# Five weight steps in six slots instead of seven, two a slot in the first sixteen, and one empty step behind each weight load

## The chip, the core and the metric

The kernel runs on one core of a Trainium2 chip. The metric is the device time of one execution in microseconds (us). The kernel before was run three times: 621.59, 623.79 and 624.48 us, median 623.79 us.

## What is computed

The reference is an attention with a hash mask, followed by a gated convolutional feed-forward layer:

```
q_bucket, k_bucket = sign bits of q @ proj and k @ proj, as numbers
scores = where(q_bucket == k_bucket, scale * q @ k.T, -1e9)
attn   = softmax(scores);  x = attn @ v          # B 4, H 8, S 768, D 64
gate   = sigmoid(causal conv of x, 5 taps, conv_w)
out    = (gate * (x @ w_val)) @ w_out            # 512 x 512 weights
```

`w_val`, `w_out` and `conv_w` come as 64-bit floats, which the chip's engines don't compute with. The kernel reads them as pairs of 32-bit integers and converts each weight into a high part and a low part of single precision (`wv[0]`, `wv[1]`, `wo[0]`, `wo[1]`), since the products are made of three partial products (high by high, high by low, low by high).

## The kernel before

**Units and slots.** There are 32 units (4 batches by 8 heads), and each has six tiles of 128 queries, 192 tiles in all. The main loop (L490) takes one pass per tile; a pass is called a slot here, and slot k is the pass that computes the exponentials of tile k (L290). In the slot, in this order: ScalarE (ACT) copies the transposed probabilities of tile k-4 out of PSUM (L323); VectorE (DVE) takes the row maxima of tile k (L272) and two small factors (L278, L282); GpSimd (POOL) normalises tile k-2 (L305); TensorE (PE) computes the scores of tile k+1 (L266); ACT computes the exponentials; then come the steps of the side work, and at the end PE transposes tile k-3 (L314). In odd slots PE also multiplies by the values (L337).

**Order.** The order on PE, ACT, DVE and POOL is the order in which the program is written (`manual_schedule`); each engine runs its list strictly in that order, and an instruction that waits holds all behind it. The score tiles have two PSUM buffers, so the scores of tile k+2 wait for the exponentials of tile k. The transposed tiles have two buffers (`tp`), and one tile uses both, so the transposes of a slot wait for ACT's copies of the tile before. SyncE (SP) issues the transfers in a list of its own, also in order.

**Side work.** Generators stand beside the loop, and each `yield` ends a step: `prep` builds the operands of the next unit (POOL L170 and L173, then transfers between partitions, L174 to L182), `early_bits` computes hash bits of later units (L221 loads, L226, L229), `pair_x` does the convolution on DVE (L368), and `load_weights` (L131) converts the weights. There are two `load_weights` generators, which take turns: `weights[0]` first converts `conv_w` and then the parts 0, 2, 4, 6; `weights[1]` converts the parts 1, 3, 5, 7. Parts 0 to 3 are the quarters of `w_val`, parts 4 to 7 those of `w_out`. The first step of each generator runs ahead of the loop.

**The steps of a part.** One part is 128 x 512 values. Its steps are: the load (L137, 512 KB); ACT's absolute value, which is the transfer's first reader (L91); two DVE operations (L93, L94); one DVE operation (L97); two DVE operations (L100, L101); a DVE cast (L109); a POOL subtraction (L111); a POOL addition (L113) and, in the same step, the load of this generator's next part. That is seven steps a part. The loads have two buffers in turn: part 0 takes the second one fresh, and part 3 takes the buffer of part 1 when L113 of part 1 is done. The slots take 1, 0, 2, 0, 2, 2 steps in turn (L515), seven in six slots, and the last step of a part falls in slot 56.

Of the kernel before, what the change touches and what calls it, by code (L numbers as in the profile page):

```python
# [26 lines left out]
def kernel(  # L27
# [11 lines left out]
    B, H, _, S = qk.shape  # L39
# [65 lines left out]
    def split_weight(w, hi, lo):  # L105
        if w.dtype == I32:
            a, d = yield from from_float64(w, op.tile([P, 512], FP32, name="o"))
            yield
            nc.vector.tensor_copy(out=hi, in_=a)  # L109
            yield  # L110
            nc.gpsimd.tensor_tensor(out=a, in0=a, in1=hi.bitcast(FP32), op=ALU.subtract)  # L111
            yield
            nc.gpsimd.tensor_tensor(out=lo, in0=a, in1=d, op=ALU.add)  # L113
        else:
            nc.scalar.copy(out=hi, in_=w)
            yield
            nc.gpsimd.tensor_tensor(out=lo, in0=w, in1=hi.bitcast(FP32), op=ALU.subtract)

    def load_conv():
        if conv_w.dtype == mybir.dt.int64:  # L120
            w = const.tile([P, NP * KW, 2], I32, name="cw64")
            nc.sync.dma_start(out=w, in_=conv_w.bitcast(I32).rearrange("p (n t) -> p n t", t=2))
            t = const.tile([P, NP * KW], FP32, name="cwt")
            yield
            a, d = yield from from_float64(w, t)
            yield
            nc.vector.tensor_tensor(out=cw_sb, in0=d, in1=a, op=ALU.add)
        else:
            nc.sync.dma_start(out=cw_sb, in_=conv_w)

    def load_weights(which):  # L131
        parts = [(src[:, c, :], hl[0][:, c, :], hl[1][:, c, :])
                 for src, hl in ((w_val, wv), (w_out, wo)) for c in range(NP)]
        for src, hi, lo in parts[which::2]:
            if src.dtype == mybir.dt.int64:
                w = wst.tile([P, 512, 2], I32, name="w64")
                nc.sync.dma_start(out=w, in_=src.bitcast(I32).rearrange("p (n t) -> p n t", t=2))  # L137
            else:
                w = wst.tile([P, 512], FP32, name="w32")
                nc.sync.dma_start(out=w, in_=src)  # L140
            yield
            yield from split_weight(w, hi, lo)

    def load_raw(i):
        if i < len(units):
            b, h = units[i]
            raws[i] = raw.tile([P, S], FP32, name="r")
            nc.sync.dma_start(out=raws[i], in_=qk[b, h])

    def load_values(i):  # L150
        b, h = units[i]
        if h % 2 == 0:
            vts[i] = vp.tile([P, KB, P], FP32, name="vt")
            nc.sync.dma_start(out=vts[i], in_=v[b, h // 2])
        else:
            vts[i] = vts[i - 1]
# [81 lines left out]
    def first_prep():  # L238

        r = raws[0]  # L240
        aq, ak, bq, bk = stacks[0] = [stk.tile([P, S], FP32R, name=nm) for nm in ("aq", "ak", "bq", "bk")]
        z = ps_t.tile([P, 512], FP32, name="tp")
        for g in range(4):
            nc.tensor.matmul(out=z[32 * g:32 * g + 2 * NB, 0:HS], lhsT=proj_sb[:, 2 * NB * (g // 2):2 * NB * (g // 2 + 1)],
                             rhs=r[:, HS * (g % 2):HS * (g % 2 + 1)], start=True, stop=True, tile_position=(0, 32 * g))
        nc.scalar.copy(out=aq[0:D], in_=r[0:D])
        nc.vector.tensor_copy(out=bk[D:P], in_=r[D:P])
        nc.vector.tensor_copy(out=ak[0:D], in_=r[D:P])
        nc.gpsimd.tensor_tensor(out=bk[0:D], in0=r[D:P], in1=bk[D:P].bitcast(FP32), op=ALU.subtract)
        for g in (0, 2, 3, 1):  # L250
            if g == 1:
                nc.vector.tensor_tensor(out=bq[D:P], in0=r[0:D], in1=aq[0:D].bitcast(FP32), op=ALU.subtract)  # L252
            nc.vector.tensor_scalar(out=(aq, ak)[g // 2][D:M, HS * (g % 2):HS * (g % 2 + 1)],
                                    in0=z[32 * g:32 * g + 2 * NB, 0:HS],
                                    scalar1=rows_sb[32 * g:32 * g + 2 * NB, 2:3],
                                    scalar2=rows_sb[32 * g:32 * g + 2 * NB, 3:4], op0=ALU.is_ge, op1=ALU.mult)
        nc.scalar.copy(out=bq[0:D], in_=r[0:D])
# [218 lines left out]
    with tc.manual_schedule(engines=ENGINES):  # L476
        for i in range(5):
            load_raw(i)
        load_values(0)
        first_prep()  # L480
        weights = [[load_conv(), load_weights(0)], [load_weights(1)]]
        preps = [first_bits(), prep(1)]
        scores(0)
        next(preps[1])
        step(preps)
        step(weights[0])
        step(weights[1])
        ahead = [early_bits()]
        turn = 0
        for k in range(N + LAG + 1):  # L490
            if 0 <= k - LAG - 1:
                keep_transposed(k - LAG - 1)
            pair = k % 2 == 0 and 0 <= k - 2 < N
            if k < N:
                maxima(k)
            if pair:
                row_sums(k - 2)
            if k < N:
                factors(k)
            if pair:  # L500
                recip(k - 2)
            if 0 <= k - 2 < N:
                normalise(k - 2)
            if k < N:
                shifts(k)
            if k + 1 < N:
                if tiles[k + 1][0] != tiles[k][0]:
                    finish(preps)
                    preps = [prep(tiles[k + 1][0] + 1)]
                scores(k + 1)  # L510
            if k < N:
                exponentials(k)
            if k >= 60 or k % 2:
                step(convs)
            for _ in range((1, 0, 2, 0, 2, 2)[k % 6]):  # L515
                step(weights[turn])
                turn = 1 - turn

            thin = k // 6 % 8 in (7, 0) and k < 186
            for _ in range(3 if cur["gates"] else (1, 0)[k % 2] if thin else 1):  # L520
                step(moes)
            cur["gates"] = max(0, cur["gates"] - 1)
            step(preps)
            if 6 <= k < 60 and k % 6 in (2, 4):
                step(ahead)
            if k % 2:
                step(avs)
                step(avs)
            if 0 <= k - LAG < N:
                transposes(k - LAG)  # L530
        accs[:] = [(ps_m, "m"), (ps_t, "tp"), (ps_s, "s"), (ps_t, "tp"), (ps_s, "s")]
        finish(avs)
        cur["gates"] = 0
        cur["end"] = True
        while convs:
            step(convs)
            step(moes)
        finish(moes)
# [59 lines left out]
```

## Time and profile before

| | |
|---|---|
| median of three runs | 623.79 us |
| span of the profiled execution, first to last instruction | 620.8 us |
| that is below the three runs by | 0.8 to 3.7 us, 3.0 us below the median |
| busy: PE, DVE, ACT, POOL | 94%, 70%, 68%, 64% of the span |

The page gives no time of its own for the profiled execution beside the span; what lies around the span is taken as the 3.0 us to the median. Slot 0 begins at 12.05 us, slot 16 at 53.80, slot 53 at 157.30, slot 65 at 188.48 (the start of L290 in each). The first use of the weights on PE is at 188.1 us (L399), of the output weights at 224.9 us (L424).

### The profile page before, as it was taken

The page shows a single profiled execution, that of the slowest core. Times are in us where ns is not written, and L with a number is a line of the kernel's source. Part 1 is how long each engine was busy: PE and PEld are TensorE (multiplying, and loading weights), DVE is VectorE, ACT ScalarE, POOL GpSimd, SP SyncE. Part 2 cuts the span into 40 slices and gives each one's busy share as a digit, 9 for nine tenths or more (in the row PEclk, how much of TensorE's full clock was granted, in tenths as well). Part 3 has the DMA queues.
Part 4 walks back from the last instruction along what each step waited for, and adds up shares of the span by engine and source line. Part 5 has one row for each costly group of instructions (what it writes and reads, how often), then busy time and mean ns, then how long its engine had stood idle before and what let it go on. Part 6 is the DMA issues. An engine that isn't in the chain of part 4 may idle for free.

```text
span 620.8 us, 10648 instructions
## 1 busy us (share of the span) xinstructions
PE 585.5 (94%) x3496; PEld 423.4 (68%) x3496; DVE 437.6 (70%) x1017; ACT 421.4 (68%) x881; POOL 395.6 (64%) x373
## 2 busy tenths in 40 slices
PE   5789898989999999999999999999999999999997
PEld 2655565555657777776767777777667877775895
DVE  5869798998975866668575867569665877665532
ACT  2777777778778666777787676777787766765400
POOL 3576868778766765578564777568764777544321
PEclk9799999999999999999999999999999999999999
DMA  6467666564532235243433234333422213200111
GB/s 227 123 197 199 200 167 208 157 175 118 133 83 68 70 79 142 72 108 82 122 82 107 61 80 126 84 115 82 108 70 78 67 42 91 69 18 1 51 52 51
DMA packets 29031, 64.64 MB, mean 104 GB/s; under 512 B 4937, under 2 KB 10057, under 8 KB 28977
## 3 DMA queue, kind: packets, MB, share of 16 engines
q1 hardware_dynamic: 28832, 63.93, 37.8%
q8 instruction: 28, 0.46, 0.3%
q14 instruction: 27, 0.21, 0.1%
q10 hardware_dynamic: 144, 0.03, 0.0%
HBM read 30.60 MB, written 7.86 MB: 62 GB/s over the span
## 4 chain that ended last, share of the span: by engine, by line
PE 66%; DVE 12%; ACT 12%; DMA 5%; issue 3%; POOL 2%; SPq 1%; ACTq 0%; POOLq 0%; DVEq 0%
PE av L337 17%; PE s L266 16%; PE tp L314 12%; PE m L424 8%; PE m L399 7%; ACT p L290 5%; DVE nm L272 4%; ACT pt L323 3%; ACT x L345 2%; DMA w<-in_w_val_dram 2%; DVE g L368 2%; PE tp L399 1%; PE tp L424 1%; PE s L424 1%; DMA bk<-bq 1%
## 5 line engine op out<-in xcount | busy, mean ns | idle before, releaser
L305 POOL TENSOR_SCALAR p<-p,ri 128x768 f32<-128x768 f32 x192 | 210.5, 1100 | 156.0 <-DVE nb L282 130.8
L272 DVE TENSOR_REDUCE nm<-s 128x1 f32<-128x768 f32 x192 | 182.5, 950 | 61.2 <-PE s L266 61.0
L290 ACT ACTIVATE p<-s,nb,gs 128x768 f32<-128x768 f32 x192 | 192.6, 1003 | 46.2 <-DVE nb L282 41.9
L323 ACT COPY pt<-tp 128x384 f32<-128x384 f32 x384 | 165.7, 485 | 75.3 <-PE tp L314 74.4
L314 PEld LDWEIGHTS tp<-ident,p 128*128 128x128 f32 x1152 | 130.3, 142 | 72.2 <-issue 43.6
L314 PE MATMUL tp<-ident,p 128*128 128x128 f32 x1152 | 164.4, 279 | 2.6 <-ACT pt L323 2.1
L337 PE MATMUL av<-pt,vt 128*64 128x384 f32 x768 | 144.9, 498 | 0.0
L266 PE MATMUL s<-ak,aq 76*128 76x384 f32 x384 | 118.1, 389 | 23.2 <-ACT p L290 19.7
L266 PE MATMUL s<-bk,bq 128*128 128x384 f32 x384 | 101.3, 345 | 0.4 <-DVE bq L252 0.4
L337 PEld LDWEIGHTS av<-pt,vt 128*64 128x64 f32 x768 | 47.0, 136 | 61.5 <-issue 61.4
L266 PEld LDWEIGHTS s<-ak,aq 76*128 76x128 f32 x384 | 59.2, 194 | 38.7 <-ACT p L290 34.6
L368 DVE SCALAR_TENSOR_TENSOR g<-x,cw_sb,g 128x768 f32<-128x768 f32 x64 | 79.4, 1241 | 2.2 <-POOL g L366 2.1
L266 PEld LDWEIGHTS s<-bk,bq 128*128 128x128 f32 x384 | 71.7, 194 | 0.8 <-issue 0.8
L173 POOL TENSOR_TENSOR bq<-r,aq 128x768 fp32r<-128x768 f32 x31 | 59.2, 1909 | 0.1
L410 POOL TENSOR_TENSOR hl<-ht,hh 128x384 fp32r<-128x384 f32 x32 | 32.3, 1009 | 39.5 <-DVE hh L408 39.5
L345 ACT COPY x<-av 64x384 f32<-64x384 f32 x64 | 30.4, 475 | 29.7 <-PE av L337 29.0
L282 DVE TENSOR_SCALAR nb<-nm,gs 128x1 f32<-128x1 f32 x192 | 40.4, 211 | 3.5
L399 PE MATMUL m<-xh,wv 128*128 128x384 f32 x200 | 42.7, 337 | 0.0
L358 POOL TENSOR_TENSOR xl<-x,xh 128x384 fp32r<-128x384 f32 x32 | 33.4, 1059 | 13.8 <-DVE xh L357 13.8
L290 ACT ACTIVATION_READ_ACCUMULATOR p<-s,nb,gs 128x1 f32 x192 | 39.0, 203 | 0.0
L404 DVE TENSOR_TENSOR ht<-m,g 128x384 f32<-128x384 f32 x25 | 13.9, 556 | 35.6 <-PE m L399 29.2
L424 PE MATMUL m<-wo,hh 128*128 128x512 f32 x144 | 38.1, 394 | 0.0
(86 smaller groups left out, 486.9 us busy)
## 6 DMA issues: line engine op xcount, KB each, us to landing
r<-in_qk_dram SPq DMA_DIRECT2D x32, 384.0 KB
vt<-in_v_dram SPq DMA_DIRECT2D x16, 384.0 KB
out_dram<-o SPq DMA_DIRECT2D x24, 256.0 KB
ak<-aq SPq DMA_DIRECT2D x31, 192.0 KB
bk<-aq SPq DMA_DIRECT2D x31, 192.0 KB
bk<-bq SPq DMA_DIRECT2D x31, 192.0 KB
bq<-aq SPq DMA_DIRECT2D x31, 192.0 KB
hh<-in_qk_dram SPq DMA_DIRECT2D x16, 192.0 KB
```

Source lines behind the costliest of these rows:

```text
L173: nc.gpsimd.tensor_tensor(out=bq, in0=r, in1=aq.bitcast(FP32), op=ALU.subtract)
L266: nc.tensor.matmul(out=s[:, hf, 0:HS], lhsT=lq[0:n, qs], rhs=rk[0:n, hf * HS:(hf + 1) * HS], start=n == M, stop=n == P)
L272: nc.vector.tensor_reduce(out=nm, in_=s[:, :, 0:HS], axis=AX.XY, op=ALU.max, negate=True)
L290: nc.scalar.activation(out=p, in_=s[:, :, 0:HS], func=AF.Exp, bias=nb, scale=gs.pop(k), accum_out=sm[:, k % 2, 0:1])
L305: nc.gpsimd.tensor_scalar(out=p, in0=p, scalar1=rcs.pop(k), scalar2=1.0, op0=ALU.mult, op1=ALU.mult)
L314: nc.tensor.transpose(out=tp[:, n * P:(n + 1) * P], in_=p[:, kb * P:(kb + 1) * P], identity=ident)
L323: nc.scalar.copy(out=pt[:, :, qo:qo + P], in_=tp[:, 0:HS].rearrange("p (a b) -> p a b", b=P))
L337: nc.tensor.matmul(out=av[s * D:(s + 1) * D, 0:HS], lhsT=vt[:, kb, hh * D:(hh + 1) * D], rhs=pt[kb // 3][:, kb % 3, :], start=(kb == 0), s ...
L345: nc.scalar.copy(out=x[hh * D:(hh + 1) * D, o:o + HS], in_=av[s * D:(s + 1) * D, 0:HS])
L368: nc.vector.scalar_tensor_tensor(out=g, in0=x[:, k:k + S], scalar=w, in1=g, op0=ALU.mult, op1=ALU.add)
L399: nc.tensor.matmul(out=acc[:, 0:HS], lhsT=wv[wi][:, c, j * P:(j + 1) * P], rhs=xs_[(c, o)][xi], start=(m == 0), stop=(m == 11))
L424: nc.tensor.matmul(out=acc, lhsT=hs[(o, j)][hi][:, tb * P:(tb + 1) * P], rhs=wo[wi][:, j, :], start=(m == 0), stop=(m == 11))
```

## The change

The conversion takes two steps a slot in slots 0 to 15, and from slot 16 on 1, 0, 1, 1, 1, 1 in turn, five in six slots. Behind the load of a part stands a second `yield`, an empty step, so that a part has eight steps and the reader L91 comes one step of its generator later after the load. All lines behind L141 move down by one.

```
@@ -138,6 +138,7 @@
                 w = wst.tile([P, 512], FP32, name="w32")
                 nc.sync.dma_start(out=w, in_=src)
             yield
+            yield
             yield from split_weight(w, hi, lo)
@@ -512,7 +513,7 @@
             if k >= 60 or k % 2:
                 step(convs)
-            for _ in range((1, 0, 2, 0, 2, 2)[k % 6]):
+            for _ in range(2 if k < 16 else (1, 0, 1, 1, 1, 1)[k % 6]):
                 step(weights[turn])
                 turn = 1 - turn
```

Counted out slot by slot, the steps fall like this (only DVE's operations, ACT's L91 and the loads are listed; the number is the part):

```
slot   before                        after
 4     L93/94 of 1                   load 0; L100/101 of 1
 6     L100/101 of 1                 L91 of 0; L111 of 1
 7     -                             L93/94 of 0; L113 of 1; load 3
 8     load 0; L109 of 1             L97 of 0
 9     -                             L100/101 of 0; L91 of 3
10     L91 of 0; L111 of 1           L109 of 0; L93/94 of 3
11     L93/94 of 0; L113, load 3     L111 of 0; L97 of 3
12     L97 of 0                      L113 of 0; load 2; L100/101 of 3
14     L91 of 3; L100/101 of 0       L91 of 2; L111 of 3
15     -                             L93/94 of 2; L113 of 3; load 5
...
20     load 2; L109 of 3             L91 of 5
22     L91 of 2; L111 of 3           L93/94 of 5
26     L91 of 5; L100/101 of 2       L113 of 2; load 4
53     L111 of 6                     L113 of 7
59     -                             L109 of 6
64     -                             L113 of 6, the last step
```

Nothing is added or removed on an engine; PE's list is the same.

ACT in slots 8 to 10, before: L91 here reads `w_425`, part 0.

```order
L290 ACTIVATE p,sm<-s,nb,gs 128x768
L323 COPY pt<-tp 128x3x128 x2
L290 ACTIVATE p,sm<-s,nb,gs 128x768
L323 COPY pt<-tp 128x3x128 x2
L290 ACTIVATE p,sm<-s,nb,gs 128x768
L91 ACTIVATE o<-w_425 128x512
L323 COPY pt<-tp 128x3x128 x2
```

And after, slots 8 to 10, where L91 reads `w_405`, part 3:

```order
L291 ACTIVATE p,sm<-s,nb,gs 128x768
L324 COPY pt<-tp 128x3x128 x2
L291 ACTIVATE p,sm<-s,nb,gs 128x768
L91 ACTIVATE o<-w_405 128x512
L324 COPY pt<-tp 128x3x128 x2
L291 ACTIVATE p,sm<-s,nb,gs 128x768
L324 COPY pt<-tp 128x3x128 x2
```

The L91 whose load stands in this place of SP's list (between `bq<-aq` of unit 2 and the four loads `hh`) comes behind the exponentials of slot 10 before, and behind those of slot 9 after.

POOL from slot 5 on, before: L173 builds `bq` of unit 2, `p` is the normalisation, `w_176` is part 1.

```order
L170 CAST aq<-r 128x768
L305 TENSOR_SCALAR p<-p,ri 128x768
L173 TENSOR_TENSOR bq<-r,aq 128x768
L305 TENSOR_SCALAR p<-p,ri 128x768 x4
L111 TENSOR_TENSOR w_176<-w_176,wv_120 128x512
L305 TENSOR_SCALAR p<-p,ri 128x768
L113 TENSOR_TENSOR wv_121<-w_176 128x512
```

And after:

```order
L171 CAST aq<-r 128x768
L306 TENSOR_SCALAR p<-p,ri 128x768
L111 TENSOR_TENSOR w_176<-w_176,wv_120 128x512
L174 TENSOR_TENSOR bq<-r,aq 128x768
L306 TENSOR_SCALAR p<-p,ri 128x768
L113 TENSOR_TENSOR wv_121<-w_176 128x512
L306 TENSOR_SCALAR p<-p,ri 128x768 x4
```

The subtraction of part 1 now stands ahead of `bq` of unit 2. SP's list around it is, before, `bk<-bq`, `aq<-u`, `r`, `bq<-aq`, load of part 0, four loads `hh`; after, the same with the load of part 3 in that place, and the load of part 0 stands further ahead, in front of `vt` of unit 2.

DVE in slots 40 and 41, before: `w_1333` is part 4, `w_1453` part 7, `g` the convolution.

```order
L93 TENSOR_SCALAR o<-o 128x512
L94 TENSOR_SCALAR o<-o 128x512
L109 CAST wo_122<-w_1333 128x512
L229 TENSOR_SCALAR ht<-m,packed 128x384
L272 TENSOR_REDUCE nm<-s 128x1
L278 TENSOR_SCALAR gs<-nm 128x1
L282 TENSOR_SCALAR nb<-nm,gs 128x1
L368 SCALAR_TENSOR_TENSOR g<-x,cw_sb,g 128x768
L97 SCALAR_TENSOR_TENSOR w_1453<-w_1453,o 128x512
```

And after:

```order
L109 CAST wo_122<-w_1118 128x512
L230 TENSOR_SCALAR ht<-m,packed 128x384
L273 TENSOR_REDUCE nm<-s 128x1
L279 TENSOR_SCALAR gs<-nm 128x1
L283 TENSOR_SCALAR nb<-nm,gs 128x1
L369 SCALAR_TENSOR_TENSOR g<-x,cw_sb,g 128x768
L93 TENSOR_SCALAR o<-o 128x512
L94 TENSOR_SCALAR o<-o 128x512
```

L93 and L94 of part 7 moved from in front of the row maxima of tile 41 to behind the convolution of slot 41, and L97 left this place for slot 44.

## Rows read from the trace of the kernel before

**Rows 1.** The page, part 1: busy us, share of the span, instructions.

```profile
PE 585.5 (94%) x3496; PEld 423.4 (68%) x3496; DVE 437.6 (70%) x1017; ACT 421.4 (68%) x881; POOL 395.6 (64%) x373
```

**Rows 2.** Busy us by stretch: length, PE, PEld, DVE, ACT, POOL, clock, DMA share, GB/s.

```profile
18.90:25.70 6.80, 6.40 (x24) 6.21 (x25) 5.96 (x16) 5.29 (x12) 3.91 (x5) 0.50 0.50 152
27.57:53.80 26.23, 22.95 (x147) 14.87 (x144) 20.49 (x53) 20.25 (x45) 17.91 (x17) 1.00 0.67 183
53.80:157.30 103.50, 92.85 (x594) 58.31 (x594) 92.68 (x208) 77.43 (x166) 83.14 (x76) 1.00 0.60 169
157.30:188.48 31.18, 29.16 (x191) 18.90 (x188) 26.67 (x60) 24.00 (x52) 21.99 (x21) 1.00 0.43 107
300.00:400.00 100.00, 98.79 (x590) 73.06 (x588) 68.63 (x164) 73.68 (x153) 64.84 (x62) 1.00 0.37 97
```

**Rows 3.** Waits of slots 16 to 52: us in total, times, longest.

```profile
ACT p L290 <- DVE nb L282: 12.3, 19, 1.6
...
PE s L266 <- ACT p L290: 9.0, 13, 1.8
```

**Rows 4.** ACT's L91, the loads' first reader: its idle time by releaser.

```profile
  DMA w<-in_w_val_dram: 3.3, 2
  DMA w<-in_w_out_dram: 0.5, 1
```

**Rows 5.** DVE operations of the conversion: ns minimum, median, maximum; starts; forms.

```profile
L93 DVE TENSOR_SCALAR o<-o x8: 416/426/1194, 22.3 to 140.3; 128x512 f32<-128x512 f32 x8
L94 DVE TENSOR_SCALAR o<-o x8: 427/1018/1024, 22.7 to 141.5; 128x512 int32<-128x512 int32 x8
L97 DVE SCALAR_TENSOR_TENSOR w<-w,o x8: 680/890/1318, 25.1 to 143.8; 128x512 int32<-128x512 int32 x8
L100 DVE TENSOR_SCALAR o<-w x8: 416/576/827, 27.4 to 147.7; 128x512 int32<-128x512 int32 x8
L101 DVE SCALAR_TENSOR_TENSOR w<-w,o x8: 1273/1276/1281, 27.8 to 148.5; 128x512 f32<-128x512 uint32 x8
...
L109 DVE CAST wv<-w x4: 409/416/419, 32.1 to 87.2; 128x512 fp32r<-128x512 f32 x4
```

**Rows 6.** Timeline of ACT, slots 9 to 11: start, us, what, idle before.

```profile
35.03 0.19 ACT L290 ACTIVATION_READ_ACCUMULATOR p<-s,nb,gs 128x1 f32 x1
...
39.77 0.69 ACT L91 ACTIVATE o<-w 128x512 f32<-128x512 f32 x1 [1.62 <-DMA w<-in_w_val_dram]
40.37 0.85 ACT L323 COPY pt<-tp 128x384 f32<-128x384 f32 x2
```

**Rows 7.** Timeline of POOL and of SP's issues, slots 6 to 10.

```profile
28.55 2.25 POOL L173 TENSOR_TENSOR bq<-r,aq 128x768 fp32r<-128x768 f32 x1
...
30.82 0.48 SPq L176 DMA_DIRECT2D bk<-bq  x1
...
33.92 0.58 SPq L137 DMA_DIRECT2D w<-in_w_val_dram  x1
...
36.70 1.30 POOL L111 TENSOR_TENSOR w<-w,wv 128x512 f32<-128x512 f32 x1
```

**Rows 8.** Timeline of PE, scores and transposes of slot 10, transposes of slot 11.

```profile
36.78 0.52 PE L266 MATMUL s<-bk,bq 128*128 128x384 f32 x2
...
37.14 0.82 PE L314 MATMUL tp<-ident,p 128*128 128x128 f32 x6
...
40.98 0.84 PE L314 MATMUL tp<-ident,p 128*128 128x128 f32 x6 [0.37 <-ACT pt L323]
```

**Rows 9.** Timeline: L94 of two parts, and what POOL ran around them.

```profile
22.38 2.17 POOL L305 TENSOR_SCALAR p<-p,ri 128x768 f32<-128x768 f32 x2 [2.51 <-DVE nb L282]
...
22.75 1.02 DVE L94 TENSOR_SCALAR o<-o 128x512 int32<-128x512 int32 x1
...
39.83 0.82 POOL L170 CAST aq<-r 128x768 fp32r<-128x768 f32 x1
...
40.97 0.43 DVE L94 TENSOR_SCALAR o<-o 128x512 int32<-128x512 int32 x1
```

More of the change, by code (lines that the diff above doesn't have):

```diff
@@ L140, in load_weights @@
                 nc.sync.dma_start(out=w, in_=src)
+            yield
             yield
@@ L514 @@
                 step(convs)
-            for _ in range((1, 0, 2, 0, 2, 2)[k % 6]):
+            for _ in range(2 if k < 16 else (1, 0, 1, 1, 1, 1)[k % 6]):
                 step(weights[turn])
```

## The prediction, made before the changed kernel ran

> **What bounds the kernel now.** I read the page first: PE is busy 94% of the span, the others 64 to 70% [rows 1]. So a change off PE can only give back what PE idles, and the question is where it idles. The table by stretch answers that [rows 2]. From 300 to 400 us PE is busy 98.79 of 100 us: nothing to win there. In slots 16 to 52 (53.80 to 157.30 us), while the conversion runs, PE is busy 92.85 of 103.50 us and DVE 92.68, almost as much. In slots 53 to 64, with the conversion all but over, PE is busy 29.16 of 31.18 us (93.5%) and DVE 85.5%. The waits of slots 16 to 52 say how DVE holds PE: the exponentials waited for DVE's factor nb 19 times, 12.3 us, and PE's scores waited for exponentials 13 times, 9.0 us [rows 3]. The circle is short: row maxima, factors, exponentials, then the score buffer is free for the tile after next. A conversion operation that stands between two row maxima lengthens it. The second thing to see is ACT's wait on the weight transfers: 3.3 us in two waits for w_val, 0.5 us for w_out [rows 4]. In such a wait ACT also holds up the copies and exponentials behind it. The engine that decides here is thus DVE from slot 16 on; before, it is the order around the first loads.
>
> **The change, part by part.** The DVE work of one part, at median durations, is 0.43 + 1.02 + 0.89 + 0.58 + 1.28 + 0.42 = 4.62 us [rows 5]; eight parts make 37 us. The change moves it between three stretches.
>
> Up to slot 15, DVE before has done part 1 and part 0 without the cast, 4.62 + 4.20 = 8.8 us; after, parts 1, 0 and 3 and the first two operations of part 2, 13.86 + 1.45 = 15.3 us. That is 6.5 us more. In slots 16 to 52, before, come one cast and six parts, 0.42 + 27.7 = 28.1 us; after, the rest of part 2, three parts and two operations of part 6, 3.17 + 13.86 + 1.45 = 18.5 us, so 9.7 us less. Behind slot 53 lie 3.2 us that were not there.
>
> *Gain, slots 16 to 52.* DVE's 92.68 us fall to 83.0. If PE then reaches the share that it has in slots 53 to 64, where DVE is busy 85.5%, its 92.85 us of work take 92.85 / 0.935 = 99.3 us instead of 103.5: 4.2 us won. Two of ACT's three waits on weight loads lie in this stretch too (all but the 1.62 us of slot 10 [rows 6]), and go: from slot 16 on a load is four or five slots ahead of its reader. Bounds: no change of share gives 0; the 98.8% of 300 to 400 us would give 94.0 us, 9.5 us won. I take 4.2, because the stretch with nearly that DVE load and the same convolution is the nearest row, and keep 2 to 6.5.
>
> *Loss, slots 53 to 64.* DVE goes from 26.67 to 29.9 of 31.18 us, the load at which PE has its 90% share in slots 16 to 52. At that share 29.16 us take 32.4 us, 1.2 us more. Since only slots 54, 57 and 59 are hit, I take 1.0 (0 to 2).
>
> *Loss, slots 0 to 15, first half.* Slots 1 to 8 get 2.3 us more DVE work (8.6 against 6.3 us, at the same medians). The half-clock stretch from 18.90 to 25.70 us leaves DVE only 6.80 - 5.96 = 0.84 us idle [rows 2]. So about 1.2 us of it comes through as a lag of the whole circle (0 to 2.3).
>
> *Loss, slots 0 to 15, second half.* Here one moved step drags a transfer. POOL's subtraction L111 of part 1, 1.30 us [rows 7], now stands ahead of bq of unit 2. Before, that bq ended at 28.55 + 2.25 = 30.80 us; after, 1.2 + 1.30 us later, at 33.3. SP issues bk<-bq at its end, and waits for it before bq<-aq, and only then the weight load: 3.12 us from the end of bq to the load's issue at 33.92 [rows 7]. So the load of part 3 goes out at 36.4, and with the 5.85 us that the load in this place took (33.92 to 39.77, where its reader starts [rows 6, 7]) it is there at 42.25. Its reader now stands behind the exponentials of slot 9, not of slot 10; those ended at 35.22 us, so at 36.4 with the lag. ACT waits 5.8 us, where it waited 1.62 [rows 6]. Behind the reader (0.69 us) are the copies of tile 6, which free the buffers for PE's transposes in slot 10. These began at 37.14 us before [rows 8]; now at about 42.25 + 0.69 + 0.45 = 43.4. PE has the scores of slot 10 left and is done with them about 1.2 us after the 37.3 us of before [rows 8], at 38.5, and idles 4.9 us. Before, the wait of 1.62 us cost PE only 0.37 us directly [rows 8], since scores and values stood in its list; that comes back. DVE, whose L93 of part 3 waits for the reader as well, stands still too, and in a stretch in which it needs 20.49 + 4.2 = 24.7 of 26.23 us that can't be made up. So 1.2 + 4.9 - 0.4 = 5.7 us, less some catching up (PE idled 26.23 - 22.95 = 3.3 us in this stretch before [rows 2]); I take 5.0. Bounds: without the lag and with half a wait, 2.5; with a lag of 2.3 and a wait of 1.7 us at slot 14, where the load of part 2 is also two slots ahead of its reader, 7.5.
>
> *Free edits.* The load of part 0 now goes out ahead of vt of unit 2: 0.33 us on SP, covered since vt is first read some twelve slots later; its reader in slot 6 falls in a stretch where ACT is busy 20.25 of 26.23 us [rows 2]. L113 and L111 of part 0 stand ahead of operands of unit 3 that are due in slot 17. The empty steps issue nothing.
>
> A price that may be lower: L94 took 1.02 us at 22.75 us, while POOL normalised, and 0.43 us at 40.97, just after POOL had ended [rows 9]. The Trainium skill (GPSIMD Engine Reference, section Specifications) says that POOL's way into SBUF is shared with DVE and contended by DVE's two-port modes; the trace agrees for this operation. By the cheap price three early L94 would save 1.8 us of the 6.5; by the medians nothing. I stay with the medians, as POOL is fuller after the change, not emptier.
>
> **Sum.** 5.0 - 4.2 + 1.0 = +1.8 us on a span of 620.8, so 622.6; with the 3.0 us between this span and the median of the runs, 625.6 us. A measurement of this kernel can tell about 0.5% (3.1 us) from no change, so this is "no change", with a lean to slower.
>
> **The rivals.**
>
> *The half clock comes back: slower.* PE's idle stretch of nearly 5 us at slot 10 would be the longest after the start. The granted clock was 0.50, the lower of the two levels, from 18.90 to 25.70 us, behind a start with long gaps, and 1.00 in every later row [rows 2]. If it falls again, a stretch of the same 6.8 us costs 3.4 us of PE work: 1.8 + 3.4 = +5.2, 629.0 us. It decides from the point where PE stands still for several us. For it: no gap of this length is in the trace, so nothing shows that the clock survives one. Against: the gap may be split by the scores and values left. The Trainium skill (TensorE: Matmul & The Clock Gate, section HAM oscillation) tells of a kernel that fell back to half clock at each wait for a transfer; no row here shows a wait that long.
>
> *The reader does not wait: faster.* If the load of part 3 lands by the time of its reader (bq less late, or the transfer quicker), the early loss is the lag alone: 1.2 - 4.2 + 1.0 = -2.0 us; with the upper end of the gain, 6.5, it is -4.3. I put it at -3.3, 620.5 us. For it: there are two slots between load and reader, about 5.2 us at the pace of these (26.23 us for ten), against 5.85 us of flight, and DVE's 24.7 us fit into 26.23. Against: the load is issued behind the same transfers as before, and its reader comes a slot sooner.
>
> *The conversion was not what held DVE: slower.* If the convolution and the hash bits alone keep the exponentials late, the gain doesn't come: +5.0 and no more, 628.8 us. Against it: DVE's busy share falls together with the conversion's end [rows 2].
>
> **How the numbers follow.** Forecast 0.47, with a range of its own of 622 to 629; half clock 0.14; no wait 0.28; no gain 0.11. Faster by more than 3.1 us (under 620.7): 0.21 of "no wait" and 0.04 of the forecast, 0.25. Slower by more (over 626.9): 0.14 + 0.09 + 0.12 of the forecast, 0.35. Within: 0.40. The range from 618.8 (near the far end of "no wait", 619.5, less the spread of the runs) to 630.5 (half clock and a larger early loss) leaves out 2 in 10.
>
> **What would show it.** Right: ACT's wait before L91 of part 3 over 4 us, PE idle at slot 10 for over 3 us, and slot 16 starting 4 to 6 us later than 53.80; from there to slot 53 under 101 us, DVE's busy share there near 84%, and no wait of ACT on a weight load. Wrong: slot 16 at 55 us or sooner (no wait), a granted clock under 1.00 behind 30 us (half clock), or slots 16 to 52 still at 103 us (no gain). Nothing behind slot 65 should change; a difference there would mean that the order of the transfers matters later than I think.

## The result and the profile after

The changed kernel takes 631.74 us (median), the kernel before 623.79 beside it: ratio 1.014, 95% interval 1.0121 to 1.0159. So it is slower by 8 us by the medians and by 9.1 us by the two profiled executions (spans 629.9 and 620.8 us), where the forecast was 625.6 us and the range ended at 630.5. Slot numbers and slot starts are those of above; every line behind L141 is one higher than before.

The page of the kernel after, part 1 (busy us, share of the span, instructions):

```profile
PE 591.1 (94%) x3496; PEld 424.8 (67%) x3496; DVE 444.0 (70%) x1017; ACT 420.8 (67%) x881; POOL 393.0 (62%) x373
```

Against [rows 1] PE has 5.6 us more busy time with the same 3496 instructions: some of them ran longer. Busy time by stretch, after (length, PE, PEld, DVE, ACT, POOL, granted clock, DMA share, GB/s), from the start of slot 6 to that of 16, then 16 to 53, 53 to 65, 33 to 36, 57 to 60, and deep behind the conversion:

```profile
27.94:59.09 31.15, 26.55 (x158) 15.72 (x156) 27.98 (x57) 20.99 (x47) 22.15 (x21) 0.95 0.65 170
59.09:162.28 103.19, 93.22 (x588) 58.74 (x586) 87.63 (x196) 76.27 (x164) 74.49 (x71) 0.98 0.58 163
162.28:197.67 35.39, 30.83 (x192) 19.64 (x189) 30.00 (x64) 24.06 (x53) 22.35 (x21) 0.95 0.36 89
103.85:115.57 11.72, 8.27 (x44) 5.11 (x41) 9.18 (x19) 5.50 (x12) 8.52 (x8) 0.85 0.62 194
172.80:184.51 11.71, 8.29 (x44) 5.23 (x41) 8.61 (x19) 5.51 (x12) 7.22 (x8) 0.85 0.36 92
300.00:400.00 100.00, 98.55 (x593) 73.25 (x593) 68.06 (x165) 73.95 (x154) 67.37 (x64) 1.00 0.34 91
```

The clock column is the first surprise: 0.95, 0.98 and 0.95 in the three stretches that had 1.00 before [rows 2]. The last row is as before. Cut by the starts of the slots (L290 of before, L291 of after, in the timeline), the time went like this, in us:

| stretch | before | after | difference |
|---|---|---|---|
| to slot 16 | 53.80 | 59.09 | +5.3 |
| 16 to 33 | 47.48 | 44.76 | -2.7 |
| **33 to 36** | 8.34 | 11.72 | **+3.4** |
| 36 to 57 | 58.22 | 57.23 | -1.0 |
| **57 to 60** | 7.57 | 11.71 | **+4.1** |
| 60 to 65 | 13.07 | 13.16 | +0.1 |
| behind 65 | the same within 0.1 | | 0 |

Six slots out of 192 hold +7.5 us. The rest is an early loss of 5.3 us, against a gain of 3.6 us in the other slots from 16 on. The six slots in the kernel before (columns as above):

```profile
101.28:109.62 8.34, 7.65 (x50) 5.20 (x47) 7.14 (x19) 6.30 (x14) 7.18 (x8) 1.00 0.67 211
167.84:175.41 7.57, 6.71 (x44) 4.58 (x41) 5.30 (x16) 5.51 (x13) 5.81 (x7) 1.00 0.38 104
```

**Slot 33.** The timeline of after, DVE's, POOL's, ACT's and PE's operations from slot 33 on (start, duration, engine, line, operation; in brackets the idle time before and its releaser):

```profile
103.67 1.01 DVE L369 SCALAR_TENSOR_TENSOR g<-x,cw_sb,g 128x768 f32<-128x768 f32 x1
104.59 0.62 DVE L358 CAST xh<-x 128x384 fp32r<-128x384 f32 x2
105.13 1.23 DVE L93 TENSOR_SCALAR o<-o 128x512 f32<-128x512 f32 x1
106.40 1.10 DVE L94 TENSOR_SCALAR o<-o 128x512 int32<-128x512 int32 x1
107.42 0.94 DVE L273 TENSOR_REDUCE nm<-s 128x1 f32<-128x768 f32 x1
...
105.03 2.19 POOL L359 TENSOR_TENSOR xl<-x,xh 128x384 fp32r<-128x384 f32 x2 [1.42 <-DVE xh L358]
...
109.18 0.99 ACT L291 ACTIVATE p<-s,nb,gs 128x768 f32<-128x768 f32 x1 [3.10 <-DVE nb L283]
...
110.31 0.62 PE L267 MATMUL s<-ak,aq 76*128 76x384 f32 x2 [3.45 <-ACT p L291]
...
111.23 2.83 PE L338 MATMUL av<-pt,vt 128*64 128x384 f32 x8
```

In this slot DVE has the last convolution step of a pair of heads and the two casts of `x` behind the factors of tile 33. The kernel before runs no conversion step in such a slot (its table has 0 at remainder 3 of 6). After, L93 and L94 stand there as well, so the row maxima of tile 34 begin at 107.42 us. They also take long here, 1.23 and 1.10 us (the least in [rows 5] is 0.42 and 0.43): each ends 0.3 us behind one of POOL's two subtractions `xl`, which the casts release. ACT waits 3.10 us for nb, PE 3.45 us for the exponentials. Then the second half of the price: eight `av` products take 2.83 us, where undisturbed ones take 1.51. Slot 57 is the same with L100 and L101:

```profile
179.25 0.89 PE L267 MATMUL s<-ak,aq 76*128 76x384 f32 x2 [3.42 <-ACT p L291]
```

The clock of the stretches behind these two stops, and of one in the early part:

```profile
36.05:39.47 3.42, 3.42 (x12) 1.12 (x10) 3.18 (x9) 1.34 (x3) 1.07 (x2) 0.50 0.89 228
111.15:114.56 3.41, 3.41 (x12) 1.35 (x12) 1.98 (x6) 0.84 (x2) 3.02 (x4) 0.50 0.63 188
179.41:182.82 3.41, 3.41 (x12) 1.64 (x12) 2.10 (x6) 1.52 (x4) 1.99 (x3) 0.50 0.25 54
```

PE is busy all through them at 0.50, the lower level. Half of the three stretches is 5.1 us, an estimate of what they add to PE's busy time, out of the 5.6 us by which it grew.

**The early part.** The timeline of after around slots 7 to 10 (POOL, DVE, PE, ACT):

```profile
29.98 2.01 POOL L174 TENSOR_TENSOR bq<-r,aq 128x768 fp32r<-128x768 f32 x1
...
29.61 0.70 DVE L93 TENSOR_SCALAR o<-o 128x512 f32<-128x512 f32 x1
30.34 1.93 DVE L94 TENSOR_SCALAR o<-o 128x512 int32<-128x512 int32 x1
...
35.62 0.66 PE L267 MATMUL s<-ak,aq 76*128 76x384 f32 x2 [1.64 <-ACT p L291]
...
36.84 2.79 PE L338 MATMUL av<-pt,vt 128*64 128x384 f32 x8
...
34.48 0.99 ACT L291 ACTIVATE p<-s,nb,gs 128x768 f32<-128x768 f32 x1 [2.41 <-DVE nb L283]
...
40.38 0.68 ACT L91 ACTIVATE o<-w 128x512 f32<-128x512 f32 x1 [2.92 <-DMA w<-in_w_val_dram]
```

The wait for the load of part 3 is there (2.92 us, against 1.62 before). But a first stop comes two slots earlier: L94 takes 1.93 us beside POOL's `bq`, ACT waits 2.41 us for nb, and slot 8 begins 2.25 us later than before (34.48 us against 32.23). Behind it the clock falls.

### The profile page after: what moved, and what is told of

Read it like the earlier page. It is cut to its first block, busy times and chain, and to the rows that moved or that the text cites. A ratio compares the mean times of both kernels' runs of the same rounds, so it can differ in the third digit from the quotient of the medians.

```text
span 629.9 us, 10651 instructions
## 1 busy us (share of the span) xinstructions
PE 591.1 (94%) x3496; PEld 424.8 (67%) x3496; DVE 444.0 (70%) x1017; ACT 420.8 (67%) x881; POOL 393.0 (62%) x373
## 4 chain that ended last, share of the span: by engine, by line
PE 68%; DVE 14%; ACT 12%; DMA 3%; issue 2%; POOL 0%; SPq 0%; ACTq 0%; POOLq 0%; DVEq 0%
PE av L338 18%; PE s L267 17%; PE tp L315 12%; PE m L425 8%; PE m L400 6%; ACT p L291 6%; DVE nm L273 4%; ACT pt L324 3%; ACT x L346 2%; DVE g L369 2%; DMA w<-in_w_val_dram 2%; PE tp L400 1%; PE tp L425 1%; PE s L425 1%; DVE o L94 1%
## 5 line engine op out<-in xcount | busy, mean ns | idle before, releaser
L306 POOL TENSOR_SCALAR p<-p,ri 128x768 f32<-128x768 f32 x192 | 208.3, 1089 | 164.7 <-DVE nb L283 137.6
L291 ACT ACTIVATE p<-s,nb,gs 128x768 f32<-128x768 f32 x192 | 192.6, 1003 | 55.3 <-DVE nb L283 49.2
L338 PE MATMUL av<-pt,vt 128*64 128x384 f32 x768 | 148.6, 509 | 0.0
L283 DVE TENSOR_SCALAR nb<-nm,gs 128x1 f32<-128x1 f32 x192 | 40.4, 210 | 3.7 <-DVE ri L301 0.2
L291 ACT ACTIVATION_READ_ACCUMULATOR p<-s,nb,gs 128x1 f32 x192 | 39.0, 203 | 0.0
```

What stands on the lines that cost most here:

```text
L291: nc.scalar.activation(out=p, in_=s[:, :, 0:HS], func=AF.Exp, bias=nb, scale=gs.pop(k), accum_out=sm[:, k % 2, 0:1])
L306: nc.gpsimd.tensor_scalar(out=p, in0=p, scalar1=rcs.pop(k), scalar2=1.0, op0=ALU.mult, op1=ALU.mult)
L338: nc.tensor.matmul(out=av[s * D:(s + 1) * D, 0:HS], lhsT=vt[:, kb, hh * D:(hh + 1) * D], rhs=pt[kb // 3][:, kb % 3, :], start=(kb == 0), s ...
```

## The experiments

The theory from this profile: the forecast terms hold, and two slots in which the new table adds a two-operation step to an already crowded slot cost the rest. Rivals: the time is the early part's; the empty step's; or that of DVE's sum, wherever the work stands. The kernel before ran beside each group of runs at 622.6 us; ratios are to it.

**Each part of the change alone.** The empty step alone, in the kernel before:

```diff
             yield
+            yield
             yield from split_weight(w, hi, lo)
```

> Edit: the kernel before with the empty step alone; the table stays 1, 0, 2, 0, 2, 2. Theory (pile-up): the 8 us come from slots in which two DVE operations of the conversion stand behind the last convolution step and the casts of the next pair (slots 33 and 57), each with a drop of the granted clock, and from the crowded slots 7 to 10. This kernel has none of them: no step falls into the slots that leave 3 by 6, and there are three slots between a load and its reader instead of two, so ACT's 3.8 us of waiting on weight loads go. 622 to 624.5 us, clock 1.00 from 30 us on. Rival (the empty steps themselves cost, since they push the conversion's end from slot 56 to slot 62): 625 to 627 us.

Measured: 625.07 us, 1.0058 [1.0037, 1.0080]. That is the rival's number. The reader's move does what it should: ScalarE's waits before L91 shrink from 3.8 to 0.4 us, and slot 29 comes 4.7 us earlier than in the kernel before. But eight empty steps push all later steps back, and in slot 29 L100 and L101 land behind a convolution step. The timeline of this kernel:

```profile
85.17 1.09 DVE L369 SCALAR_TENSOR_TENSOR g<-x,cw_sb,g 128x768 f32<-128x768 f32 x1
86.18 1.04 DVE L100 TENSOR_SCALAR o<-w 128x512 int32<-128x512 int32 x1
87.26 0.69 DVE L101 SCALAR_TENSOR_TENSOR w<-w,o 128x512 f32<-128x512 uint32 x1
...
90.49 0.61 PE L267 MATMUL s<-ak,aq 76*128 76x384 f32 x2 [2.22 <-ACT p L291]
...
91.38 2.83 PE L338 MATMUL av<-pt,vt 128*64 128x384 f32 x8
```

It is much the same picture as in slot 33: a PE stop, then the half clock (91.40 to 94.81 us). From slot 29 to 53 this kernel loses 3.6 us of its lead. Another 3.2 us are lost from slot 53 to 65, where steps now run that were done before slot 56. My expectation was missed: moving the reader later by an empty step is not free.

The early rate alone, and the late table alone (both with the empty step):

```diff
-            for _ in range((1, 0, 2, 0, 2, 2)[k % 6]):
+            for _ in range(2 if k < 16 else (1, 0, 2, 0, 2, 2)[k % 6]):
```

```diff
-            for _ in range((1, 0, 2, 0, 2, 2)[k % 6]):
+            for _ in range((1, 0, 2, 0, 2, 2)[k % 6] if k < 16 else (1, 0, 1, 1, 1, 1)[k % 6]):
```

> Edit: the changed kernel with the old table from slot 16 on, so only slots 0 to 15 and the empty steps are new. Theory (pile-up): the early part alone costs 5.3 us up to slot 16, as in the changed kernel (slot 16 at about 59 us), with one drop of the clock at 36 us; behind it no step falls into slots 33 and 57, no second or third drop, and with 6.5 us less DVE work left it wins back 1 to 3 us: 626 to 628 us. Rival (the late spread is harmless and the whole loss is early): 631 to 632 us. Second rival (the early part is made up by slot 65): 622 to 624 us.

Measured: 626.14 us, 1.0065 [1.0045, 1.0085]; slot 16 comes 5.0 us late, and slots 33 to 36 and 57 to 60 take 8.5 and 7.6 us. So the early loss is there without the late table.

> Edit: the changed kernel with the old table in slots 0 to 15, so only the slots from 16 on and the empty steps are new. Slot 45 gets L100/L101 behind the convolution and the casts, slot 21 gets L93/L94 behind the casts alone, slots 33 and 57 get a POOL and an ACT step. Theory (pile-up): one stall of 3 to 4 us at slot 45 with a drop of the clock, at most 1.5 us at slot 21, slot 16 at 53 to 54 us, a gain of 2 to 4 us in the other slots: 622.5 to 626 us. Rival (the early part is the whole loss): 619 to 621 us, the thinner spread wins. Second rival (the late end of the conversion, here slot 82, costs whatever the slot): 628 us or more.

Measured: 629.20 us, 1.0124 [1.0098, 1.0150]; slot 16 comes 2.9 us earlier than before, and all is lost later. The steps fall otherwise here: L100 and L101 land in slot 45, again one with the convolution step and two casts, PE stops for 3.42 us before 138.43, and a half-clock stretch follows from 139.26. In slot 21 L93 and L94 behind the two casts alone stop PE for 2.27 us, and another such stretch follows from 70.99, more than I expected there. Steps that run past slot 57 lose another 3.9 us (slots 60 to 65 take 16.94 us, before 13.07), and 1.8 us are lost behind slot 65, as the last step falls in slot 82. So the late table loses by itself, partly in the crowded slots where its steps fall; but the time is that of the second rival, and here a late end of the conversion costs as well.

**The two slots.** First the table with another slot free, 0 steps at remainder 3 of 6 and a step at remainder 1:

```diff
-            for _ in range(2 if k < 16 else (1, 0, 1, 1, 1, 1)[k % 6]):
+            for _ in range(2 if k < 16 else (1, 1, 1, 0, 1, 1)[k % 6]):
```

> Edit: the changed kernel with 1, 1, 1, 0, 1, 1 in place of 1, 0, 1, 1, 1, 1, so that the free slot of the six is the one with the convolution's last step and the casts. Theory (pile-up): slots 33 and 57 run in 2.5 to 3.5 us instead of 5.3, without a drop of the clock behind them; that gives back 3.4 + 4.1 us: 623 to 626 us, the early 5.3 us stay. Rival (the rate or the end of the conversion, not the slot, makes the loss): 630 to 632 us, with stalls elsewhere. Second rival (only the clock falls by itself): the stalls go but the clock still falls twice, 628 us.

Measured: 625.27 us, 1.0053 [1.0033, 1.0072], some 6 us less than the changed kernel (6.5 by the medians, 5.8 by the profiled spans), at the same rate. From slot 33 to 36 it takes 7.85 us, from 57 to 60 7.57, and the clock stays at 1.00 there. That run moved steps in other slots as well. The cleanest run moves the steps of slots 33 and 57 alone, by one slot:

```diff
-            for _ in range(2 if k < 16 else (1, 0, 1, 1, 1, 1)[k % 6]):
+            for _ in range(2 if k < 16 or k in (34, 58) else 0 if k in (33, 57) else (1, 0, 1, 1, 1, 1)[k % 6]):
```

> The changed kernel with the steps of slots 33 and 57 alone listed one slot later (slots 34 and 58 run two), all else as it was. On VectorE this puts L93/L94 of slot 33 and L100/L101 of slot 57 behind the row maximum of the next tile and not ahead of it, and moves nothing else of weight. Theory (the pile-up of convolution step, two casts and a two-operation step ahead of one row maximum is what cost slots 33 and 57): slots 33 to 36 take about 8.3 us again instead of 11.7 and slots 57 to 60 about 7.6 instead of 11.7, no half clock there, time 624 to 626. Rival (the VectorE work costs the same wherever it stands in these stretches): the wait reappears before the tile after, slots 33 to 36 and 57 to 60 stay above 10.5 us each, time 629.5 to 632.

Measured: 624.27 us, 1.0029 [1.0017, 1.0041]. The timeline of slot 33 in this kernel:

```profile
104.53 1.01 DVE L369 SCALAR_TENSOR_TENSOR g<-x,cw_sb,g 128x768 f32<-128x768 f32 x1
105.46 0.62 DVE L358 CAST xh<-x 128x384 fp32r<-128x384 f32 x2
106.00 0.95 DVE L273 TENSOR_REDUCE nm<-s 128x1 f32<-128x768 f32 x1
...
107.30 0.88 DVE L93 TENSOR_SCALAR o<-o 128x512 f32<-128x512 f32 x1
108.21 1.02 DVE L94 TENSOR_SCALAR o<-o 128x512 int32<-128x512 int32 x1
...
108.89 0.61 PE L267 MATMUL s<-ak,aq 76*128 76x384 f32 x2 [1.16 <-ACT p L291]
```

And its busy time in slots 33 to 36 and 57 to 60 (columns as above):

```profile
104.71:112.94 8.23, 7.07 (x47) 4.93 (x44) 8.12 (x20) 5.72 (x12) 6.41 (x7) 1.00 0.74 229
170.13:178.13 8.00, 6.95 (x44) 4.57 (x41) 7.80 (x19) 5.59 (x13) 5.22 (x6) 1.00 0.34 97
```

L93 and L94 stand one row maximum later, the maximum begins 1.47 us after the start of the convolution step instead of 3.75, PE idles 1.16 us instead of 3.45, and the clock stays. Two pairs of DVE instructions, moved past five others each, are worth 7.5 us by the medians, and 7.2 us by the two stretches of the profiles. The rival (DVE's sum decides) falls for these slots.

**How much of it is the clock.** The changed kernel with PE kept busy in the two stops:

```diff
+            if k in (34, 58):
+                f = ps_m.tile([P, 512], FP32, name="m")
+                for _ in range(18):
+                    nc.tensor.transpose(out=f[:, 0:P], in_=ident, identity=ident)
```

> Edit: the changed kernel with 18 transposes of the identity into a PSUM tile that nobody reads, at the end of slots 34 and 58, where PE stands still for 3.4 us. The work is no part of the result; it fills about 2.5 us of each stall. Theory (the stall itself makes the granted clock fall, and the half clock behind it is a price of its own): the clock stays at 1.00 at 111 and 179 us, the products with the values behind the stall take 1.5 us instead of 2.5 to 2.8, each stall costs 1.3 to 1.8 us less: 628 to 629.5 us. Rival (the clock falls for another reason, or costs nothing since DVE is behind anyway): 631 to 633 us.

Measured: 629.17 us, 1.0096 [1.0064, 1.0129]. The timeline of the first stop, and the clock of both stretches:

```profile
104.64 0.82 PE L315 MATMUL tp<-ident,p 128*128 128x128 f32 x6
105.30 2.13 PE L535 MATMUL m<-ident 128*128 128x128 f32 x18
108.94 0.62 PE L267 MATMUL s<-ak,aq 76*128 76x384 f32 x2 [1.52 <-ACT p L291]
...
109.84 1.51 PE L338 MATMUL av<-pt,vt 128*64 128x384 f32 x8
```

```profile
102.47:112.61 10.14, 8.62 (x62) 6.55 (x59) 9.21 (x19) 5.51 (x13) 6.94 (x7) 1.00 0.57 184
169.84:179.96 10.12, 8.64 (x62) 6.54 (x59) 8.62 (x19) 5.50 (x12) 6.20 (x7) 1.00 0.31 86
```

The wait for the exponentials is as long as it was, but the useful work behind it runs at full clock: 10.1 instead of 11.7 us, twice. So of the +3.4 and +4.1 us, 1.6 us each is the clock and the rest the wait itself.

**The early part.** Two runs take one suspect each out of the kernel with remainder 3 free. No step in slot 7, so that L94 doesn't stand beside `bq`:

```diff
-            for _ in range(2 if k < 16 else (1, 1, 1, 0, 1, 1)[k % 6]):
+            for _ in range(0 if k == 7 else 2 if k < 17 else (1, 1, 1, 0, 1, 1)[k % 6]):
```

> Edit: the changed kernel with 1, 1, 1, 0, 1, 1 late, and no step in slot 7 (the two missing ones come in slot 16). L93/L94 of part 0 then run in slot 8, not beside POOL's long L174 (bq of unit 2), and the reader of load 3 stands behind the exponentials of slot 10. Theory (the early loss begins where L94 waits for POOL's L174, 1.93 us instead of 0.43 to 1.02, and the clock falls behind that): exponentials 8 start at 31.5 to 32.5 us instead of 33.6, no drop of the clock at 36 us, slot 16 at 55 to 57 us instead of 58.8; 621.5 to 624 us. Rival (the sheer DVE work of slots 0 to 15 is too much wherever it stands): slot 16 at 58 us or later, 625 us.

Measured: 623.13 us, 1.0008 [0.9991, 1.0026], the same as the kernel before. Slot 8 begins at 32.23 us instead of 33.57 (34.48 in the changed kernel) and the half clock at 36 us is gone, as expected of the theory. But slot 16 is still 4.5 us late, as expected of the rival: ScalarE waits for two loads, 1.98 us in slot 10 and 2.19 us in slot 15. Between them it waits 1.80 us for nb at slot 14, and a half-clock stretch begins at 53.21. What made this run fast lies behind: from slot 16 to 53 it takes 98.7 us, against 103.5 before and 101.5 with remainder 3 free alone. Slot 16 makes up one of the two steps that slot 7 lost, not both as the expectation says, so every later step stands one place later; why that gives 2.9 us no run shows.

And two more empty steps for part 3, so that its reader doesn't wait:

```diff
-        for src, hi, lo in parts[which::2]:
+        for n, (src, hi, lo) in enumerate(parts[which::2]):
...
             yield
             yield
+            if which == 1 and n == 1:
+                yield
+                yield
```

> Edit: the kernel of the run with 1, 1, 1, 0, 1, 1 and two more empty steps behind the load of part 3, so that its reader stands behind the exponentials of slot 11 instead of 9; slot 7 stays as it is. Theory (the wait on the load is the second half of the early loss): the wait of 3.6 us goes, slot 12 starts 2 us or more sooner than 47.9, slot 16 at 56 to 57 us instead of 58.8; the drop of the clock at 36 us stays. Rival (L94 behind POOL is all of the early loss, the wait is hidden behind the slow clock): slot 16 at 58 to 59 us. The shift puts two-operation steps into the odd slots 31 and 37, which the first theory prices at 1 to 2 us each, so the total is 624 to 627 us.

Measured: 625.67 us, 1.0049 [1.0030, 1.0068]. The wait before L91 is gone, slot 12 begins 1.9 us earlier than with remainder 3 free alone, slot 16 1.4 us earlier, and still 3.6 us late; the first stop stays (slot 8 begins at 33.86 us), and so does a half-clock stretch, from 33.68 to 40.51 us. The difference of 1.4 us is not clear of the spread: five of the kernels here have the same order up to slot 16, and in their profiles it begins between 57.75 and 59.84 us. So each of the two runs took one suspect away and kept the other, and most of the loss stayed; no run took both, so the cause of the early loss stays open. That DVE has too little room in these slots fits as well (the conversion's operations take 16.5 us of DVE up to slot 16 here, 9.3 in the kernel before), but no run shows it by itself, since none took work out of them without moving it somewhere else.

**Looking for a faster kernel.** The kernel before with a rule instead of a table: from slot 8 on, pairs (L93/L94, L100/L101) in even slots only and one to a slot, and everywhere a reader at least four slots behind its load. The heart of the edit:

```diff
-            for _ in range((1, 0, 2, 0, 2, 2)[k % 6]):
-                step(weights[turn])
-                turn = 1 - turn
+            pairs = 0
+            for _ in range((1, 1, 2, 0, 2, 1)[k % 6]):
+                for w in (turn, 1 - turn):
+                    if kind[w] == "pair" and k >= 8 and (k % 2 or pairs) or kind[w] == "read" and k < loaded[w] + 4:
+                        continue
...
```

> Edit: the kernel before with another choice of steps: no empty steps; 1, 1, 2, 0, 2, 1 steps a slot; from slot 8 on the two-operation steps (L93/L94 and L100/L101) only in even slots, one a slot; and a load's reader not before the fourth slot behind the load. Theory (the price of a step is where it stands: behind the convolution in odd slots, beside a long POOL operation, or too close behind its load): no drop of the clock behind 30 us, no wait of ACT on weight loads, slots 16 to 65 in 132 us or less, 617 to 621 us, faster than both. Rival (rate and totals decide): 622 to 625 us, like the kernel before, which has the same number of steps by slot 56.

Measured: 624.95 us, 1.0032 [1.0017, 1.0048]; missed, in the rival's range. No wait before L91 is left and slot 23 comes 3.6 us earlier, but the rule packs L100, L101 and L109 into one slot (20, 32, 44), and between the starts of slots 43 and 48 it loses 4.5 us, with a half-clock stretch from 140.1 to 146.9. Then a smaller step: the kernel before, with the readers of parts 0, 2, 4, 6 (and L93/L94, L97 behind them) one slot later and nothing else moved:

```diff
-            for _ in range((1, 0, 2, 0, 2, 2)[k % 6]):
-                step(weights[turn])
-                turn = 1 - turn
+            held = ("0", "0", "10", "", "10", "10", "1", "", "01", "", "1", "01")
+            steps = ("0", "", "10", "", "10", "10", "1", "", "01", "", "01", "01") if k < 10 else held
+            for c in steps[k % 12]:
+                w = weights[int(c)] or weights[1 - int(c)]
+                step(w)
```

> The kernel before, with its own steps and rate, except that L91 of parts 0, 2, 4 and 6 is listed one slot later (slots 11, 23, 35, 47 instead of 10, 22, 34, 46) and L93/L94 and L97 of these parts one slot later with it, which also takes L93/L94 out of odd slots; nothing else of weight moves. Theory (of the reader's move only the wait for the load is worth anything, and the first run with the move alone lost its gain because the empty steps pushed the later steps into crowded slots): ScalarE's waits of 3.3 us in 2 and 0.5 us in 1 before L91 fall under 1 us together, slot 12 comes 1.5 to 2.5 us earlier, slot 24 some 3 us earlier, nothing is given back behind it, time 618.5 to 621. Rival (a steady stretch of this kernel takes its time from VectorE's sum, so that a wait that is taken away comes back as a wait for nb): what is won by slot 24 is gone by slot 60, time 622 to 625.

Measured: 623.46 us, 1.0022 [1.0003, 1.0040]; the rival's number. Slot 23 begins 3.3 us earlier, and by slot 45 it is gone. ScalarE's wait for nb from 20 to 200 us in this kernel (us, times, longest), and from its timeline one of the places:

```profile
ACT p L290 <- DVE nb L282: 23.7, 31, 1.8
```

```profile
108.80 1.82 POOL L173 TENSOR_TENSOR bq<-r,aq 128x768 fp32r<-128x768 f32 x1
...
109.28 1.89 DVE L97 SCALAR_TENSOR_TENSOR w<-w,o 128x512 int32<-128x512 int32 x1
...
116.44 0.99 ACT L290 ACTIVATE p<-s,nb,gs 128x768 f32<-128x768 f32 x1 [1.48 <-DVE nb L282]
```

No wait for a load is left, and the waits for nb, 18.3 us in 29 times in the kernel before, have grown by 5.4 us. L97 of part 4 moved from slot 36 to 37, beside `bq`, where it takes 1.89 us, and L100 and L101 behind it in slot 38 make tile 39 late: from slot 38 to 39 it took 2.69 us before and takes 3.87. In exchange for a wait on a transfer there is a wait for nb.

With L109 of these parts one slot later as well:

```diff
-            held = ("0", "0", "10", "", "10", "10", "1", "", "01", "", "1", "01")
+            held = ("0", "0", "10", "", "1", "10", "10", "", "01", "", "1", "01")
```

> The kernel with the readers one slot later, and in addition L109 of parts 0, 2, 4, 6 (and of the odd parts' L111) listed one slot later: the slots k of which k modulo 12 is 4 then hold L93/L94 alone and not L93/L94 with L109, and the next slots hold L97 and L109, then L100/L101 with L111. Theory (what counts is how much VectorE work stands ahead of one row maximum): 0 to 1.5 us less than the kernel with the readers moved alone, 617.5 to 620.5. Rival (such spreading moves a wait and saves none): within 0.7 us of that kernel.

Measured: 622.45 us, 0.9998 [0.9985, 1.0011]: the same as the kernel before, 1.0 us under the kernel without it, though the two intervals overlap, so this run doesn't decide between its theory and its rival. ScalarE's waits for nb are 25.9 us in 33 times here, more than without the move, and yet this kernel is not slower: the sum of these waits doesn't give the time. None of these versions beats the kernel before.

## Why the prediction was wrong, step by step

**The step that failed: the gain of slots 16 to 52, with the loss of slots 53 to 64.** I counted DVE's operations per stretch and turned a stretch's DVE sum into a PE share. That takes DVE's work as if it could stand anywhere in its stretch. The table of the change counts out slots 4 to 26, then 53, 59 and 64. Slot 33 stands nowhere in it, and slot 57 is named in the prediction as one of three that are hit, but priced by the share alone; what else DVE runs in these two slots I didn't list, as I did for slots 40 and 41. Slots 16 to 53 took 103.19 us, against 99.3 forecast and 103.50 before, which is what I had named as the sign that the gain is wrong; slots 53 to 65 took 35.39, +4.2 instead of +1.0. DVE's sum did fall (87.63 us, against 92.68 [rows 2]), but not to the forecast 83.0: the conversion's operations took 9.1 us less there, close to the 9.7 counted, while other DVE operations got longer (18 sums of rows, L297, from 2.89 to 5.32 us, ten convolution steps from 11.23 to 12.34). ScalarE waited for nb 17 times, 15.0 us, instead of 19 times, 12.3 us [rows 3]: fewer waits, longer ones. After, slots 16 to 52:

```profile
ACT p L291 <- DVE nb L283: 15.0, 17, 3.1
...
PE s L267 <- ACT p L291: 8.3, 10, 3.5
```

**The sizes of these terms were right without the two slots.** With the steps of slots 33 and 57 moved by one slot, slots 16 to 53 take 99.77 us and 53 to 65 32.12 us: -3.7 and +0.9, where I had -4.2 and +1.0:

```profile
59.84:159.61 99.77, 92.07 (x592) 58.17 (x591) 87.25 (x196) 76.56 (x164) 74.64 (x71) 1.00 0.59 168
159.61:191.73 32.12, 29.75 (x192) 19.10 (x189) 30.36 (x64) 24.31 (x53) 23.96 (x21) 1.00 0.39 99
```

That kernel's 624.27 us is 1.3 us from the forecast. The sum lacked one term: +7.5 us for two crowded slots. That the gain then fits is luck in part: DVE's sum fell by 5.4 us instead of 9.7, and PE's share rose to 92.3%, not 93.5%.

**The early loss, +5.0, was right in size (+5.3), but partly by luck, since its cause was partly wrong.** The load of part 3 was issued at 35.75 us (36.4 forecast), landed at 40.4 (42.25; it flew 4.6 us, not 5.85), and its reader waited 2.92 us, not 5.8. PE then idled 0.42 us at slot 10, not 4.9. Two of the signs that I named for this step were thus absent, while the third, slot 16 at +4 to +6, was there. The lag of 1.2 us didn't build up over slots 1 to 8 either: slot 7 began at 30.22 us (30.52 before), and slot 8 was 2.25 us late at once. Neither this stop nor the half clock at 36 us behind it was in the sum. How the 5.3 us divide between the stop, the wait and DVE's load no run shows.

**L94's price** went up, not down: 0.94 us on average before, 1.07 after, 1.93 in slot 7. My doubt was about the right thing (POOL as its neighbour) with the wrong sign. In the paragraph on the second half of slots 0 to 15 I had moved L111 ahead of `bq` and `bq` later with it, and so had what was needed to see that `bq` could run beside L94 of part 0.

**The rival of the half clock** came true in kind, three times and at places that I hadn't named. I let it hang on one stop of about 5 us. Stops of 1.64, 3.45 and 3.42 us were followed by it, and at an extra cost of 1.6 us each in the late two, not 3.4; no run prices the early one.

**No wait of ScalarE on a load from slot 16 on** was right: of the 3.5 us before L91 of after (3.3 and 0.5 before [rows 4]) 2.92 lie in slot 9 and 0.59 in slot 14, where the prediction's upper bound had put a second wait:

```profile
  DMA w<-in_w_val_dram: 3.5, 2
```

But the runs with the readers moved show that these waits were worth little in the end: with all of them gone the kernel before is not faster. **Nothing behind slot 65** changed, as said.

## What to carry to other kernels

When a table of steps is changed, list for each slot of the whole run what then stands between one critical operation and the next on the engine that feeds the circle, and price the worst slots, not the sum of the stretch: four instructions in the wrong two slots cost 7.5 us here, twice what the change won in all other slots from 16 on (3.6 us). A stall of PE has to be priced with what comes behind it, here a stretch at half clock. And a wait that is taken away is a gain only if the work that moves with it lands in slots with room.

## What the runs showed of the hardware

**Some DVE operations beside a long POOL operation end with it.** L94 takes 0.43 us with POOL still [rows 9], 1.02 beside the normalisation [rows 9], and 1.93 beside `bq`; when it began at 30.34, `bq` ran until 31.99, and L94 until 32.27. It is not only L94: a sum of rows over 128x2 (L297), 0.15 us at its shortest, took 1.01 us from 33.06 on beside L113, which ran from 33.01 to 34.04, and ended at 34.07. L101, 1.28 us by [rows 5], takes 0.69 where POOL stands still, as in the slot 29 shown above. The timeline of after at slot 13, where a cast that took 0.42 us elsewhere needs four times as long:

```profile
49.16 1.81 POOL L174 TENSOR_TENSOR bq<-r,aq 128x768 fp32r<-128x768 f32 x1
...
49.52 1.74 DVE L109 CAST wv<-w 128x512 fp32r<-128x512 f32 x1
```

`bq` ends at 50.97, the cast at 51.26. The row maxima (0.94 to 0.97 us over all 192) show no such thing. So the price of L94, L97 and L109 depends on their place beside POOL. The Trainium skill (Perfetto Trace Analysis, section Optimizing Scalar/DVE Operations) says that POOL's only port into SBUF is DVE's second pair, and that a DVE operation which uses two ports holds it alone; the rows agree that the two hinder each other, and here it is DVE that waits. What the port does can't be seen in a trace.

**The granted clock can fall behind a short stop, and its length alone doesn't decide.** Idle times of PE of 1.64, 2.22, 3.42 and 3.45 us were each followed by a stretch of 3.4 us at 0.50 in which PE was busy throughout, and filling the two late stops with other PE work kept it at 1.00. But a stop of 2.19 us before 132.70 in the kernel with the early rate alone kept 1.00, and with one of 1.31 us before 30.63 in the last kernel above came a stretch of 3.4 us at 0.50. In one place a stop of 1.83 us (before 127.45, in the kernel with the readers moved) was followed by such a stretch, and the kernel before has its longest, 1.84 us [rows 3], there (before 128.64) and keeps 1.00. What decides between these the runs don't show, and the kernel before, with no such stretch in the slots behind slot 6, gives no price for one.
